# Attention of a three-stage kernel: the turned sums and rows of a pair behind the next pair's first scores, VectorE's work in another order, the scores' scale in the tanh, other first loads

## The chip, the cores and the metric

The kernel runs on one core of one Trainium2 chip. The metric is the time of one execution on the device in microseconds (us), lower is better; for each kernel the median of several runs is given. A profiled execution gives the trace, whose span is a little shorter than the run's time.

## The reference

Three stages follow each other: attention with a cap on the scores, a mixture of experts in which each token goes to one expert, and a soft mixture of experts.

```python
def _attn_ref(q, k, v, cap):                 # 4 x 12 heads, 448 positions, 64 wide
    scores = 1.0 / np.sqrt(q.shape[-1]) * np.matmul(q, k.transpose(0, 1, 3, 2))
    scores = cap * np.tanh(scores / cap)
    scores = scores - np.max(scores, axis=-1, keepdims=True)
    attn = np.exp(scores)
    attn = attn / (np.sum(attn, axis=-1, keepdims=True) + 1e-09)
    return np.matmul(attn, v)

def reference(...):
    x = attn_out.transpose(0, 2, 1, 3).reshape(1792, 768)
    x = _moe_ref(x, ...)       # logits = x @ w_gate + bias; argmax; gate * relu(x @ w1[e]) @ w2[e]
    return _moe2_ref(x, ...)   # softmax over tokens, 8 x 4 slots, experts, softmax over slots
```

## The kernel before

The work around the change is the first stage. The 48 heads are taken as 24 pairs (two heads of one batch item on 128 partitions), six pairs to each of the four batch items. The order of the instructions is written by hand in `attention` (L567): each engine runs its own instructions in the order in which this loop issues them, and semaphores make it wait for the others. Only the order within an engine can therefore be chosen, and a waiting instruction holds everything behind it on its engine, the transfers on SP's queue among them.

For pair p the steps are these.

- `load_qkv` (L754) loads q, k and v of pair p + 2 by SP's queue; pair 0 and 1 are loaded before the loop, with q of pair 0 on ScalarE's queue, behind the load of the cap (L1135).
- `split_qk` (L764) makes of q and k a high and a low part for the fp32r matmuls on VectorE, and multiplies q by `qsc`, which is 1 / (8 cap). `split(p + 1)` runs in pair p.
- `scores` (L591): the scores are made transposed (keys on partitions) in blocks of 128 keys, three matmuls to each product (high by high, high by low, low by high). Block 0 has its two PSUM banks "s"; block 1 uses banks s1 and s2, the small block of the last keys (c == NKC, both heads on one set of 128 partitions) s2, and block 2 s1 and s0. ScalarE takes the tanh of each (one instruction for block 0, one for the small block, two each for blocks 1 and 2: six a pair), and `pexp` (L607) the exponential of cap times that, in two instructions a pair.
- `scores1` does blocks 0 and 1, `scores2` the small block, `scores3` block 2.
- `pv` (L641) and `pv2` (L652) multiply the probabilities of pair p - 1 by v in the single bank "o"; `post1` (L655) copies the result from there.
- `adds1`, `adds2` add the blocks for the row sums on VectorE; `fold_rest` adds the small block too for the pairs in the set `quiet` (L694), which saves eight matmuls in `post2`.
- `post2` (L499) makes row sums and gate logits of pair p - 2 by narrow matmuls (r_ps, in the bank of `ps_m`), adds a guard on VectorE, and transposes the pair's result into the bank of `ps_x` (x_ps, L514). `post3` (L517) turns the sums (rt_ps, L520), takes reciprocals, scales the logits into `tmpg` and the rows into `xr`, which frees the bank of `ps_x`, and stores the rows to `x_dram`.
- `plan` (L678) puts the routing of a batch item (`route_batch`, L262: parts s0 to s3, of many short VectorE instructions and two matmuls for the ranks) at places (pair, 0 to 2) of the pairs behind its last rows; `route(p, place)` issues what is due. For the third batch item `route_first` and the gather for the first expert follow.
- `extra` (L660) places constants; in pairs 5 to 8 it sets the tile `xg` to zero on VectorE, which `zero_c` (L482) then stores.

The banks `s0` and "o" are also lent to routing (`Lent`, L663).

## Time and profile before

| | us |
|---|---|
| median of 3 runs | 496.83 (494.43 to 497.43) |
| the profiled execution | 496.84 |
| its span in the trace | 495.1 |
| TensorE (PE) busy | 458.5, 93% |
| VectorE (DVE) busy | 290.7, 59% |
| ScalarE (ACT) busy | 248.7, 50% |

Busy times are sums over instructions whose pipelines overlap, and an average over stages: the attention, up to about 200 us, is another mixture than what follows. A row of a timeline has the start, the duration, the engine, the source line, the operation, what it writes and reads with the shape, and how many instructions of a kind are drawn together; in brackets stands how long the engine had been idle before, and who ended that. PEld is TensorE's loading of weights, which runs beside its matmuls. "issue" means that no wait is seen.

### The profile page before, as it was taken

The page shows a single profiled execution, that of the slowest core. Times are in us where ns is not written, and L with a number is a line of the kernel's source. Part 1 is how long each engine was busy: PE and PEld are TensorE (multiplying, and loading weights), DVE is VectorE, ACT ScalarE, POOL GpSimd, SP SyncE. Part 2 cuts the span into 40 slices and gives each one's busy share as a digit, 9 for nine tenths or more (in the row PEclk, how much of TensorE's full clock was granted, in tenths as well). Part 3 has the DMA queues.
Part 4 walks back from the last instruction along what each step waited for, and adds up shares of the span by engine and source line. Part 5 has one row for each costly group of instructions (what it writes and reads, how often), then busy time and mean ns, then how long its engine had stood idle before and what let it go on. Part 6 is the DMA issues. An engine that isn't in the chain of part 4 may idle for free. (4 is left out here: it accounts for less than half of the span.)

```text
span 495.1 us, 10690 instructions
## 1 busy us (share of the span) xinstructions
PE 458.5 (93%) x4081; PEld 296.9 (60%) x4081; DVE 290.7 (59%) x738; ACT 248.7 (50%) x400; POOL 66.3 (13%) x140
## 2 busy tenths in 40 slices
PE   7999999999999989799998999999998979996773
PEld 5455555555555555588775888778876845542321
DVE  3899999999999995566652545245523323001323
ACT  4988968788798876333442335334432321100312
POOL 2100000000000004024331213121012103211000
PEclk9999999999999999899999999999999978999988
DMA  6356644665453405789949997988689899999997
GB/s 186 122 109 205 217 151 128 220 219 176 127 153 102 147 21 162 261 298 353 278 143 291 303 306 231 325 285 301 203 293 332 295 374 392 417 414 412 415 414 315
DMA packets 56214, 124.96 MB, mean 252 GB/s; under 512 B 9385, under 2 KB 25456, under 8 KB 56160
## 3 DMA queue, kind: packets, MB, share of 16 engines
q1 hardware_dynamic: 53696, 117.57, 68.9%
q0 software_dynamic: 2176, 6.44, 4.8%
q8 instruction: 33, 0.54, 0.4%
q10 hardware_dynamic: 288, 0.23, 0.2%
q14 instruction: 21, 0.17, 0.1%
HBM read 112.52 MB, written 11.71 MB: 251 GB/s over the span
## 5 line engine op out<-in xcount | busy, mean ns | idle before, releaser
L861 PE MATMUL acc_ps<-xh,wh 128*128 128x468 f32 x192 | 76.5, 399 | 1.7 <-DVEq L1260 0.9
L608 ACT ACTIVATE arena<-arena,capb 128x1792 f32<-128x1792 f32 (+1 forms) x48 | 77.0, 1604 | 1.6
L107 DVE TENSOR_TENSOR arena<-arena 128x896 f32<-128x896 f32 (+1 forms) x74 | 68.0, 919 | 9.8 <-ACT arena L608 8.0
L862 PE MATMUL acc_ps<-xl,wh 128*128 128x468 f32 x192 | 72.5, 378 | 0.0
L863 PE MATMUL acc_ps<-xh,wl 128*128 128x468 f32 x192 | 72.3, 377 | 0.0
L107 DVE TENSOR_TENSOR wl<-rw,wh 128x384 fp32r<-128x384 f32 x49 | 27.3, 559 | 74.4 <-ACT wh L814 61.7
L814 ACT CAST wh<-rw 128x384 fp32r<-128x384 f32 x64 | 32.3, 508 | 58.1 <-PE acc_ps L862 31.3
L649 PE MATMUL o_ps<-arena 128*64 128x448 f32 x288 | 59.6, 548 | 0.7 <-DVE arena L657 0.6
L605 ACT ACTIVATE arena<-s_ps 128x448 f32<-128x448 f32 x96 | 46.7, 541 | 10.3 <-PE s_ps L577 10.3
L470 POOL DMA_INDIRECT xg<-x_dram,idx x16 | 17.4, 1089 | 199.0 <-PE s_ps L577 171.0
L861 PEld LDWEIGHTS acc_ps<-xh,wh 128*128 128x128 f32 x192 | 36.5, 190 | 8.0 <-ACT wh L814 1.6
L863 PEld LDWEIGHTS acc_ps<-xh,wl 128*128 128x128 f32 x192 | 36.4, 190 | 5.3 <-DVE wl L107 0.6
L982 ACT ACTIVATE h<-acc_ps 128x468 f32<-128x468 f32 x32 | 18.0, 562 | 42.6 <-PE acc_ps L863 39.1
L862 PEld LDWEIGHTS acc_ps<-xl,wh 128*128 128x128 f32 x192 | 36.7, 191 | 3.6
L649 PEld LDWEIGHTS o_ps<-arena 128*64 128x64 f32 x288 | 18.4, 136 | 30.1 <-issue 18.9
L577 PE MATMUL s_ps<-qh,kh 64*128 64x448 f32 x144 | 32.1, 433 | 1.1 <-ACT arena L605 0.4
L577 PE MATMUL s_ps<-ql,kh 64*128 64x448 f32 x144 | 27.0, 364 | 0.2 <-DVE ql L113 0.2
L577 PE MATMUL s_ps<-qh,kl 64*128 64x448 f32 x144 | 26.9, 363 | 0.1
L107 POOL TENSOR_TENSOR wl<-rw,wh 128x384 fp32r<-128x384 f32 x15 | 15.6, 1043 | 72.5 <-ACT wh L814 49.0
L910 POOL DMA_INDIRECT c_dram<-cw,icur x16 | 16.1, 1004 | 56.7 <-DVE cw L107 42.8
L577 PEld LDWEIGHTS s_ps<-qh,kh 64*128 64x128 f32 x144 | 13.9, 183 | 16.1 <-ACT arena L605 8.9
L596 ACT ACTIVATE arena<-s_ps 128x896 f32<-128x896 f32 x24 | 21.6, 899 | 2.8 <-PE s_ps L577 2.8
(272 smaller groups left out, 743.3 us busy)
## 6 DMA issues: line engine op xcount, KB each, us to landing
ring<-in_moe_w_dram SPq DMA_DIRECT2D x30, 768.0 KB
w2r<-in_moe_w2t_dram SPq DMA_DIRECT2D x32, 384.0 KB
w2r<-in_moe_w_dram SPq DMA_DIRECT2D x28, 384.0 KB
arena<-in_moe_w_dram SPq DMA_DIRECT2D x13, 768.0 KB
rw<-in_moe_w_dram SPq DMA_DIRECT2D x24, 384.0 KB
arena<-in_moe_w_dram SPq DMA_DIRECT2D x22, 384.0 KB
kr<-in_k_dram SPq DMA_DIRECT2D x24, 256.0 KB
arena<-in_v_dram SPq DMA_DIRECT2D x24, 256.0 KB
```

Source lines behind the costliest of these rows:

```text
L107: (eng or nc.vector).tensor_tensor(out=out, in0=in0, in1=in1, op=op)
L470: nc.gpsimd.indirect_dma_start(out=xg[:, i, :], out_offset=None, in_=x_dram if rows is None else x_dram[:rows], in_offset=bass.IndirectOff ...
L577: nc.tensor.matmul(o, lhsT=kk[r, k], rhs=qq[r], start=(t == 0), stop=(t == 2))
L596: nc.scalar.activation(out=dst, in_=ps[:, :, :S], func=AF.Tanh)
L605: nc.scalar.activation(out=dst[:, h], in_=ps[h], func=AF.Tanh)
L608: nc.scalar.activation(out=t, in_=t, func=AF.Exp, scale=capb)
L649: nc.tensor.matmul(o[hd], lhsT=vt[:, c, hd], rhs=pt_t[p][:, c, h] if c < 2 else pt_m[p][:, 1 + h], start=(c == 0), stop=False)
L814: nc.scalar.copy(wh, rw)
L861: nc.tensor.matmul(ps, lhsT=wh, rhs=hi[k], start=(k == 0), stop=False)
L862: nc.tensor.matmul(ps, lhsT=wh, rhs=lo[k], start=False, stop=False)
L863: nc.tensor.matmul(ps, lhsT=wl, rhs=hi[k], start=False, stop=(k == total - 1))
L982: nc.scalar.activation(out=big["h"][n % NHB], in_=acc.pop(n), func=AF.Relu)
```

## The change

In the loop of a pair, the order becomes: scores1, fold_rest, the split of the next pair, the turn of the sums and rows of pair p - 3 (`finish`, pairs 3 to 18, its turned sums mostly in the lent bank s0), routing at place 0, pv, adds2, post2, pv2, the copy of the result (post1), routing at place 1, scores2, adds1, scores3, routing at place 2. From pair 18 on the turn of pair p - 2 also comes between scores2 and scores3, as before. The routing of the first two batch items moves one pair later, and `quiet` becomes 2, 3, 4, 6, 7, 8, 12, 13, 14, 18 (it was 2, 3, 4, 6, 7, 10, 11, 12, 13, 16, 17, 18, 19). The factor `qsc` leaves the split and becomes the scale operand of the six tanh. The zeros of `xg` come by four loads from the zero row of `x_dram`, on SP's queue. At the start q of pair 0 is issued ahead of the cap, v of pair 0 behind the loads of pair 1, the split of pair 0 ahead of the constants and with k in two halves; five matmuls warm TensorE up where seven did.

```diff
@@ -593,16 +593,16 @@
             if c == 0:
                 ps = ps_s.tile([128, 2, 512], F32, tag="s", name="s_ps")
                 product([ps[:, h, :S] for h in range(2)], k, p, by_heads)
-                nc.scalar.activation(out=dst, in_=ps[:, :, :S], func=AF.Tanh)
+                nc.scalar.activation(out=dst, in_=ps[:, :, :S], func=AF.Tanh, scale=qsc)
             elif c == NKC:
                 ps = bank(2, "sl_ps")
                 product([ps], k, p, together)
-                nc.scalar.activation(out=dst, in_=ps, func=AF.Tanh)
+                nc.scalar.activation(out=dst, in_=ps, func=AF.Tanh, scale=qsc)
             else:
                 ps = [bank(1, "s1_ps"), bank(2, "s1_ps")] if c == 1 else [bank(1, "s2_ps"), bank(0, "s2_ps")]
                 product(ps, k, p, by_heads)
                 for h in range(2):
-                    nc.scalar.activation(out=dst[:, h], in_=ps[h], func=AF.Tanh)
+                    nc.scalar.activation(out=dst[:, h], in_=ps[h], func=AF.Tanh, scale=qsc)
 
         def pexp(t):
             nc.scalar.activation(out=t, in_=t, func=AF.Exp, scale=capb)
@@ -658,7 +658,7 @@
             xun[p] = xt
 
         extra = {0: late_consts, 1: call(set_guard, 1e-9 * math.exp(-CAP_SMALL)), 2: later_consts, 4: last_consts}
-        extra.update({5 + i: call(nc.vector.memset, xg[:, i], 0.0) for i in range(NT)})
+        extra.update({5 + i: call(nc.sync.dma_start, xg_all[:, i], x_dram[NTOK].partition_broadcast(128)) for i in range(NT)})
         extra[9] = zero_c
         class Lent:
 
@@ -677,9 +677,10 @@
 
         def plan(b):
 
-            p, rb = (b + 1) * NP_ + 1, route_batch(b, a2p, lent_s)
-            at = [(p, 2), (p + 1, 1), (p + 1, 2), (p + 2, 1)]
-            if b == NB1 - 1:
+            early = b == NB1 - 1
+            p, rb = (b + 1) * NP_ + (1 if early else 2), route_batch(b, a2p, lent_s)
+            at = [(p, 2), (p + 1, 0), (p + 1, 2), (p + 2, 1 if early else 2)]
+            if early:
                 f0, f1, rest, sums_, turn = route_first(a2p, lent_s, lent_o)
                 rb += [f0, f1, sums_, rest, lambda: (turn(), gather(NA, NB1 * S))]
                 at += [(p + 1, 2), (p + 2, 2), (p + 3, 1), (p + 3, 1), (p + 3, 2)]
@@ -691,9 +692,16 @@
             for f in todo.pop((p, place), ()):
                 f()
 
-        quiet = set(range(2, LAST - 3)) - {5} - {(b + 1) * NP_ + 2 + i for b in range(NB1) for i in range(2)}
+        soon = NB1 * NP_
+        quiet = set(range(2, soon + 1)) - {NP_ - 1} - {(b + 1) * NP_ + 3 + i for b in range(NB1 - 1) for i in range(3)}
         n2 = 0
         spl[0] = first_split
+
+        def finish(q, pool=ps_m):
+            post3(q, a1, pool)
+            if q % NP_ == NP_ - 1 and q < soon:
+                plan(q // NP_)
+
         for p in range(NPAIR):
             if p + 2 < NPAIR:
                 raw[p + 2] = load_qkv(a1, a1q, p + 2)
@@ -701,9 +709,13 @@
                 m2_load(n2)
                 n2 += 1
             scores1(p)
-            route(p, 0)
             if p in quiet:
                 fold_rest(p - 2)
+            if p < LAST:
+                split(p + 1)
+            if 3 <= p <= soon:
+                finish(p - 3, ps_m if (p, 0) in todo else lent_s)
+            route(p, 0)
             if p >= 1:
                 pv(p - 1)
                 adds2(p - 1)
@@ -715,23 +727,19 @@
                 post1(p - 1)
                 post2(p - 2, a1, ps_x, ps_m)
                 break
-            split(p + 1)
             if p >= 2:
                 post2(p - 2, a1, ps_x, ps_m)
-            route(p, 1)
             if p >= 1:
                 pv2(p - 1)
+                post1(p - 1)
+            route(p, 1)
             scores2(p)
             adds1(p)
-            if p >= 1:
-                post1(p - 1)
-            if p >= 2:
-                post3(p - 2, a1, ps_m)
+            if p >= soon:
+                finish(p - 2)
             scores3(p)
             if p in extra:
                 extra[p]()
-            if p >= 2 and (p - 2) % NP_ == NP_ - 1:
-                plan((p - 2) // NP_)
             route(p, 2)
         assert not todo and n2 == NRING + 1 and a1.end <= UNIT * (NRINGA - 1)
         wsplits, xpreps, more_weights = item_start()
@@ -758,20 +766,22 @@
         vt = a1.tile([128, NKC + 1, 2 * HD], F32, tag="vt", name="vt", bufs=4)
         nc.sync.dma_start(kr, kT[b, hp])
         (eng or nc.sync).dma_start(qr, qT[b, hp].rearrange("h d s -> (h d) s"))
-        nc.sync.dma_start(vt, vP[b, hp])
-        return qr, kr, vt
-
-    def split_qk(a1q, qr, kr, act=False):
+        values = call(nc.sync.dma_start, vt, vP[b, hp])
+        if eng is None:
+            values()
+        return qr, kr, vt, values
+
+    def split_qk(a1q, qr, kr, first=False):
 
         qh, ql, kh, kl = (a1q.tile([128, w], F32R, tag=n, name=n, bufs=2)
                           for n, w in (("qh", S), ("ql", S), ("kh", S + KL), ("kl", S + KL)))
-        if act:
-            nc.scalar.copy(kh, kr)
-        else:
-            nc.vector.tensor_copy(kh, kr)
-        ts(qh, qr, qsc, ALU.mult)
-        stt(ql, qr, qsc, qh.bitcast(F32), ALU.mult, ALU.subtract)
-        tt(kl, kr, kh.bitcast(F32), ALU.subtract)
+        halves = [slice(0, 2 * KC), slice(2 * KC, S + KL)] if first else [slice(0, S + KL)]
+        for c in halves:
+            (nc.scalar.copy if first else nc.vector.tensor_copy)(kh[:, c], kr[:, c])
+        nc.vector.tensor_copy(qh, qr)
+        tt(ql, qr, qh.bitcast(F32), ALU.subtract)
+        for c in halves:
+            tt(kl[:, c], kr[:, c], kh[:, c].bitcast(F32), ALU.subtract)
         return qh, ql, kh, kl
 
 
@@ -1132,18 +1142,19 @@
             return ([call(wfirst, s) for s in range(AHEAD)], [call(xprep, k, "aat"[k % 3]) for k in range(KD)],
                     lambda: [w2load(j, e_first[-1]) for j in range(NR2)])
 
-        nc.scalar.dma_start(capt, cap.partition_broadcast(128))
         nc.vector.memset(bigf, 0.0)
         nc.vector.memset(xg_all[:, 0, :256], 0.0)
         first = {0: load_qkv(a1, a1q, 0, nc.scalar)}
+        nc.scalar.dma_start(capt, cap.partition_broadcast(128))
         nc.scalar.activation(out=bigf, in_=bigf, func=AF.Tanh)
 
         warm = ps_o.tile([128, S], F32, tag="o", name="warm")
         for _ in range(NWARM):
             nc.tensor.matmul(warm[:, :256], lhsT=xg_all[:, 0, :128], rhs=xg_all[:, 0, :256], start=True, stop=True)
+        first_split = split_qk(a1q, *first[0][:2], True)
         early_consts()
-        first_split = split_qk(a1q, *first[0][:2], act=True)
         first[1] = load_qkv(a1, a1q, 1)
+        first[0][3]()
         attention(a1, a1q, a2p, first, ps_s, ps_o, ps_x, ps_m, item_start)
 
     xh, xl, ps_a = big["xh"], big["xl"], big["ps", "a"]
@@ -1520,7 +1531,7 @@
         9], "pool": [4, 5]},
 }
 NRING = 5
-NWARM = 7
+NWARM = 5
 NRINGA = 12
 NRINGB = 5
 NRING2 = 9
```

## Rows read from the trace of the kernel before

**Rows 1.** Busy time by stretch: length, PE, PEld, DVE, ACT, POOL, PEclk, DMA share, GB/s.

```profile
43.00:66.00 23.00, 22.85 (x202) 12.88 (x200) 22.20 (x49) 19.30 (x25) 0.00 (x0) 1.00 0.54 169
434.00:480.00 46.00, 36.81 (x358) 14.09 (x350) 9.94 (x22) 7.39 (x16) 5.01 (x30) 0.93 1.02 414
```

**Rows 2.** Timeline of ScalarE, first tanh of pairs 0, 2, 5, 6, 7, 14, 15, 23.

```profile
8.68 0.92 ACT L596 ACTIVATE arena<-s_ps 128x896 f32<-128x896 f32 x1 [2.82 <-PE s_ps L577]
21.22 0.90 ACT L596 ACTIVATE arena<-s_ps 128x896 f32<-128x896 f32 x1
43.67 0.90 ACT L596 ACTIVATE arena<-s_ps 128x896 f32<-128x896 f32 x1
51.35 0.90 ACT L596 ACTIVATE arena<-s_ps 128x896 f32<-128x896 f32 x1
58.82 0.90 ACT L596 ACTIVATE arena<-s_ps 128x896 f32<-128x896 f32 x1
114.08 0.90 ACT L596 ACTIVATE arena<-s_ps 128x896 f32<-128x896 f32 x1
122.15 0.90 ACT L596 ACTIVATE arena<-s_ps 128x896 f32<-128x896 f32 x1
185.28 0.89 ACT L596 ACTIVATE arena<-s_ps 128x896 f32<-128x896 f32 x1
```

**Rows 3.** Timeline of PE and PEld in pair 6 and the start of pair 7.

```profile
55.17 0.36 PE L577 MATMUL sl_ps<-qh,kl 128*128 128x448 f32 x1
55.37 0.27 PE L520 MATMUL rt_ps<-ident,arena 128*112 128x128 f32 x1
55.88 0.37 PE L577 MATMUL s_ps<-ql,kh 64*128 64x448 f32 x2
57.08 0.18 PEld L577 LDWEIGHTS s_ps<-qh,kh 64*128 64x128 f32 x2 [0.40 <-ACT arena L605]
57.59 0.36 PE L577 MATMUL s_ps<-qh,kl 64*128 64x448 f32 x2
57.88 2.48 PE L649 MATMUL o_ps<-arena 128*64 128x448 f32 x12
```

**Rows 4.** Timeline of PE in the last pair, small and third block.

```profile
188.57 0.37 PE L577 MATMUL sl_ps<-qh,kl 128*128 128x448 f32 x1
189.18 0.36 PE L577 MATMUL s_ps<-ql,kh 64*128 64x448 f32 x2
```

**Rows 5.** Groups of ScalarE instructions, shapes apart: xcount | busy, mean ns | idle.

```profile
L877 ACT COPY htok<-h_ps 117x512 f32<-117x512 f32 x20 | 11.8, 591 | 15.1 <-PE h_ps L874 14.2
L1437 ACT ACTIVATE cT<-cT_ps,rs 96x512 fp32r<-96x512 f32 x3 | 2.0, 683 | 11.3 <-PE cT_ps L1435 11.3
L608 ACT ACTIVATE arena<-arena,capb 128x1792 f32<-128x1792 f32 x24 | 43.0, 1791 | 0.8
L608 ACT ACTIVATE arena<-arena,capb 128x1344 f32<-128x1344 f32 x24 | 34.0, 1417 | 0.8
```

**Rows 6.** Timeline of VectorE in pair 6, and of PE in pair 10.

```profile
50.62 2.33 DVE L107 TENSOR_TENSOR arena<-arena 64x448 f32<-64x448 f32 x3
57.83 0.70 DVE L236 MEMSET xg<- 117x768 f32 x1
88.14 0.32 PE L520 MATMUL rt_ps<-ident,arena 128*112 128x128 f32 x1 [0.41 <-DVE arena L110]
```

**Rows 7.** Timeline of PE, pairs 6 and 7.

```profile
54.02 0.92 PE L653 MATMUL o_ps<-arena 128*128 128x448 f32 x2
61.00 0.65 PE L514 MATMUL x_ps<-ident,arena 128*112 128x128 f32 x4
```

**Rows 8.** Groups of VectorE instructions, shapes apart, 10 to 165 us.

```profile
L107 DVE TENSOR_TENSOR arena<-arena 64x448 f32<-64x448 f32 x26 | 15.9, 611 | 0.4
```

**Rows 9.** Timeline of VectorE at the first split, of PE in pair 22.

```profile
6.33 0.45 DVE L110 TENSOR_SCALAR qh<-qr,qsc 128x448 fp32r<-128x448 f32 x1 [1.06 <-DMA qr<-in_q_dram]
179.63 0.81 PE L329 MATMUL tab_ps<-bsel,a 112*32 112x117 f32 x24
```

## What the change is predicted to do

> **What bounds the kernel now.** I read the busy table by stretches first, then the starts of the pairs on ScalarE, then TensorE and VectorE inside one pair.
>
> In the attention TensorE is without a gap: 22.85 of 23 us, with VectorE at 22.20 just behind it and ScalarE at 19.30 [rows 1]. The last weights come at the rate of the transfers: in 434 to 480 us the DMA engines are full while TensorE has 36.81 of 46 us [rows 1]. That stretch starts when earlier items free their buffers, so I let a microsecond of the attention count as one of the whole, and look for the change in the attention only.
>
> The first tanh of a pair is a good clock of the pairs. The 21 pairs from number 2 to number 22 last from 21.22 to 185.28, or 164.06 us [rows 2]. A quiet pair takes 7.47 (51.35 to 58.82), one whose sums are not folded 7.68 (43.67 to 51.35), one with the ranks of a batch 8.07 (114.08 to 122.15) [rows 2]. Pairs 0 and 1 take 12.54 together, 6.27 each: nothing old is turned in them yet, and ScalarE works through [rows 2].
>
> Inside a quiet pair TensorE has one real wait. The second block of the next pair's scores needs the bank that the tanh of this pair's third block empties: the weight load at 57.08 has been idle for 0.40, released by L605 [rows 3]. The chain is scores, tanh of head 0, scores; whatever lengthens one tanh lengthens the pair.
>
> Above 21 times 7.47 = 156.87 there are 7.2 us in these pairs. TensorE's own extra work explains: eight pairs not folded (5, 8, 9, 14, 15, 20, 21, 22) at 0.21, 1.7; the ranks of three batches at 8.07 - 7.47 - 0.21 = 0.39, 1.2; the table matmuls in pair 22, 0.8 [rows 2, 9]. About 3.5 us are left, and they are waits for VectorE's queue: so in a pair after routing, the turn of the sums starts at 88.14 after TensorE's load waited 0.41 on VectorE [rows 6].
>
> **The change part by part.** Times are against this execution, 496.84 us with a span of 495.1; the median shown, 496.83, is the same.
>
> *First loads.* VectorE begins the first split at 6.33, after 1.06 us of waiting for q alone [rows 9]. q was issued on ScalarE's queue behind the cap's load (128 tiny pieces) and beside v of pair 0; now q goes first, and v after pair 1. At best the whole 1.06 goes, at worst nothing (then k's arrival binds). From q to the first tanh was 8.68 - 6.33 = 2.35 [rows 2, 9]; the new order (split with k in halves, then three small constants, which the tanh now needs) is about as long, as an estimate. I take -0.9. Two warm-up matmuls fewer cost nothing: they end before q is there. Late next is the scale, made last on VectorE.
>
> *Scale in the tanh.* Six tanh of a pair now read a [128,1] scale. The nearest rows: a copy from PSUM of 512 columns without one takes 591 ns, one with a scale operand 683, so 92 more [rows 5]. Below, zero (hidden between back-to-back instructions); above, the exp, which has such a scale: 1791 for 1792 and 1417 for 1344 columns is 0.835 a column and 295 fixed, against 591 - 427 = 164 for the plain copy, 131 more, its source being SBUF too [rows 5]. I take 0.09, the like operation from the like memory. Where it counts:
> - pairs 0 and 1, bound by ScalarE: 2 x 6 x 0.09 = +1.1 (0 to 1.6);
> - the chain scores, tanh, scores in 21 pairs: 21 x 0.09 = +1.9 (0 to 2.7). There the next scores wait for the whole instruction, so nothing hides it.
>
> Elsewhere ScalarE has room: 19.30 of 23 us [rows 1].
>
> The Trainium skill, ScalarE: Activation LUTs, section What ACT_TABLE_LOAD costs, has 93 ns for each such operand and lets back-to-back activations overlap by as much. This trace agrees on the first (92); with the second rule carried to the chain the sum would lose the +1.9, which is the first rival below.
>
> In return qh and ql lose the scalar operand: still four instructions a pair, ql now of the kind that takes 0.61 for 448 columns [rows 8]. I count nothing; VectorE isn't the bound in a quiet pair.
>
> *The turn of the sums* (rt) leaves the place between the small block's scores and the third block's, and comes after the next pair's second block. Before: last small product 55.17, second product of the third block 55.88, 0.71. Without a turn between, in the last pair: 188.57 to 189.18, 0.61, so leaving saves 0.10 only [rows 3, 4]. At the new place scores to probabilities x V took 57.59 to 57.88, 0.29; with a turn, 0.20 (55.17 to 55.37) and then 0.20 to 0.29 more, 0.11 to 0.20 longer [rows 3]. Net 0.01 to 0.10; at 0.05 in the 15 pairs 3 to 17, +0.75. Pair 2 loses one turn and pair 18 gains it.
>
> *Fewer folds.* The set `quiet` loses 10, 11, 16, 17, 19 and gains 8, 14: three folds fewer, 3 x 0.21 = +0.6 on TensorE, and 3 x 2 x 0.61 = 3.7 us less on VectorE [rows 2, 8].
>
> *VectorE's order and load.* Four memsets of 0.7 each leave it (57.83 is one [rows 6]); SP issues four loads of a zero row in their place, each behind a store and ahead of the next pair's loads. These have most of two pairs until they are split, so I take nothing; if that cover were gone, a late k would hold the split, and then the next pair's scores. The folds, split and turned rows now run while VectorE would wait, and the copy of P x V comes ahead of the first add, which frees its bank early. Routing moves a pair later, into pairs without a fold. From all this I expect most of the 3.5 to go: -2.7, with 0.8 left where routing's chain is longest (bounds 0 and -3.5).
>
> *The new close place.* TensorE's x transposes of a pair (they follow the sums) need the PSUM bank that the rows' multiply frees; that multiply stood a whole pair ahead, and now stands in the same pair. From the end of pv2, 54.02 + 0.92 = 54.94, to the next x transposes, 61.00, are 6.06, and by the terms above 6.2 after [rows 7]. In it VectorE must do a whole pair's work but for adds2 and one short operation: 57.83 - 50.62 = 7.21, less 2.33 - 2 x 0.61 = 1.11, is at most 6.1 [rows 6, 8]. It fits, barely; I take 0.
>
> **The sum:** -0.9 + 1.1 + 1.9 + 0.75 + 0.6 - 2.7 = +0.75, or 496.84 + 0.75 = 497.6 us.
>
> **The rivals.**
> 1. The scale is hidden. For it: ScalarE often has its next instruction ready. Against: the 0.40 stands in every pair on a finished tanh [rows 3]. 497.6 - 1.1 - 1.9 = 494.6.
> 2. VectorE's waits don't go (the order only moves them): 497.6 + 2.7 = 500.3. For it: the work stays near the pair's length. Against: some 2.8 + 3.7 us leave VectorE altogether.
> 3. Slower: the rows' multiply comes after TensorE wants its bank. If VectorE's chain of 6.1 is in fact 6.8 beside the room of 6.2, each of the nine folded pairs from 3 on (18 among them) loses 0.6, 5.4 in all: 503.0. It decides from a chain of about 6.7 on. Against: 6.1 counts one operation too many.
> 4. All goes well: scale hidden (-3.0), all waits gone (-0.8), a free turn (-0.75), q the full 1.06 early (-0.16): 492.9. Only with a gain that I don't see would it pass 1%.
>
> **How the numbers follow.** About 1% (5 us) is what a measurement of this kernel can tell from no change. My forecast, near 497.6, gets 0.60; rival 1 0.13, rival 2 0.11, rival 3 0.08, rival 4 0.08, of which I put 0.07 below 491.9, since unseen gains lie there. So faster 0.07, same 0.85, slower 0.08. The range 493.3 to 501.0 holds the forecast with the bounds of its costs, rivals 1 and 2, and leaves out rival 3 and most of rival 4.
>
> **What would show it.** In the profile after: a tanh of 448 columns near 0.63, of 896 near 0.99; the first tanh near 7.8 us; pairs 0 and 1 near 6.8 each; a quiet pair near 7.6; pairs after routing without the extra 0.8 to 1.0; the load of the second block's scores still released by a tanh. I am wrong if a quiet pair stays at 7.47 or below (rival 1), if x transposes wait for VectorE (rival 3), if TensorE's granted clock falls in the attention, or if the stages behind it move by another amount than the attention does.

## The result and the profile after

The changed kernel takes 500.49 us in the median of 22 runs (497.25 to 505.44), the kernel before in the same rounds 497.02 (494.43 to 501.15): a ratio of 1.0067, 95% interval 1.0046 to 1.0087. One of the 22 executions, 505.44, lies more than 1.5% above the fastest, in a slower state, and the ratio leaves it out. The kernel is slower by 3.5 us, inside the 1% that the prediction took as no change, and inside its range (493.3 to 501.0); but the forecast, 497.6, was 2.9 us too low.

The profiled execution of the changed kernel took 504.16 us with a span of 502.4. That is 3.7 us above its own median, so its trace shows more than the change. A second trace of the same kernel, from the run e12_after_again below (500.46 us, span 498.7), is put beside it wherever the two differ.

The busy line of the page, first trace (busy us, share of the span, instructions of each engine):

```profile
PE 463.4 (92%) x4101; PEld 299.9 (60%) x4101; DVE 283.6 (56%) x729; ACT 262.1 (52%) x401; POOL 67.4 (13%) x140
```

VectorE lost 7.1 us of work and ScalarE gained 13.4, nearly all of it the tanh's; neither says by itself what became of the time.

ScalarE's first tanh of a pair is the clock of the pairs again (start, duration, engine, line, operation, shapes; in brackets the idle time before and who ended it). The first fence is the first trace of the kernel after: pairs 0, 2, 7, 8, 9, 10, 20, 21, 23. The second is its second trace: pairs 0, 1, 2, 23.

```profile
7.24 1.01 ACT L596 ACTIVATE arena<-s_ps,qsc 128x896 f32<-128x896 f32 x1 [1.83 <-DVE qsc L110]
21.60 0.99 ACT L596 ACTIVATE arena<-s_ps,qsc 128x896 f32<-128x896 f32 x1
...
60.11 0.99 ACT L596 ACTIVATE arena<-s_ps,qsc 128x896 f32<-128x896 f32 x1
67.82 0.99 ACT L596 ACTIVATE arena<-s_ps,qsc 128x896 f32<-128x896 f32 x1
75.53 0.99 ACT L596 ACTIVATE arena<-s_ps,qsc 128x896 f32<-128x896 f32 x1
84.41 0.99 ACT L596 ACTIVATE arena<-s_ps,qsc 128x896 f32<-128x896 f32 x1
...
163.58 0.99 ACT L596 ACTIVATE arena<-s_ps,qsc 128x896 f32<-128x896 f32 x1
173.37 0.99 ACT L596 ACTIVATE arena<-s_ps,qsc 128x896 f32<-128x896 f32 x1
...
190.08 0.99 ACT L596 ACTIVATE arena<-s_ps,qsc 128x896 f32<-128x896 f32 x1
```

```profile
7.08 1.01 ACT L596 ACTIVATE arena<-s_ps,qsc 128x896 f32<-128x896 f32 x1 [1.78 <-DVE qsc L110]
13.89 0.99 ACT L596 ACTIVATE arena<-s_ps,qsc 128x896 f32<-128x896 f32 x1
20.68 0.99 ACT L596 ACTIVATE arena<-s_ps,qsc 128x896 f32<-128x896 f32 x1
...
189.14 0.99 ACT L596 ACTIVATE arena<-s_ps,qsc 128x896 f32<-128x896 f32 x1
```

Against [rows 2]: the first tanh comes 1.44 to 1.60 us earlier; pairs 0 and 1 take 14.36 in the first trace and 13.60 in the second, where 12.54 stood; pairs 2 to 22 take 168.48 and 168.46, where 164.06 stood. A quiet pair takes 7.71 instead of 7.47 (60.11 to 67.82). Pair 9 with the first ranks takes 8.88 (75.53 to 84.41), pair 20 with the third 9.79 (163.58 to 173.37).

The tanh themselves, grouped by form (xcount | busy, mean ns of one | idle before): first the line of the kernel before for the 448 columns, then the kernel after.

```profile
L605 ACT ACTIVATE arena<-s_ps 128x448 f32<-128x448 f32 x96 | 46.7, 541 | 10.3 <-PE s_ps L577 10.3
```

```profile
L605 ACT ACTIVATE arena<-s_ps,qsc 128x448 f32<-128x448 f32 x96 | 55.4, 629 | 4.9 <-PE s_ps L577 4.9
L596 ACT ACTIVATE arena<-s_ps,qsc 128x896 f32<-128x896 f32 x24 | 23.7, 989 | 1.8 <-DVE qsc L110 1.8
L600 ACT ACTIVATE arena<-sl_ps,qsc 128x448 f32<-128x448 f32 x24 | 15.2, 635 | 16.4 <-PE sl_ps L577 16.4
```

A tanh of 448 columns went from 541 to 629 ns, one of 896 from 0.90 us [rows 2] to 0.989: the 0.09 of the sum.

TensorE in pair 6 and at the start of pair 7, kernel after, as [rows 3] before:

```profile
56.39 0.36 PE L577 MATMUL sl_ps<-qh,kl 128*128 128x448 f32 x1
...
56.99 0.36 PE L577 MATMUL s_ps<-ql,kh 64*128 64x448 f32 x2
...
58.28 0.18 PEld L577 LDWEIGHTS s_ps<-qh,kh 64*128 64x128 f32 x2 [0.49 <-ACT arena L605]
58.79 0.37 PE L577 MATMUL s_ps<-qh,kl 64*128 64x448 f32 x2
59.09 0.32 PE L520 MATMUL rt_ps<-ident,arena 128*112 128x128 f32 x1
59.34 2.48 PE L649 MATMUL o_ps<-arena 128*64 128x448 f32 x12
```

Two things are to be seen. The wait of the weight load on the tanh of the third block is 0.49 instead of 0.40. And from the last product to the probabilities x V are 0.55 us, where 0.29 stood [rows 3]: 0.30 to the turn, 0.25 after it.

The ranks of a batch now stand ahead of the probabilities x V on TensorE. The kernel after at pair 9 and at pair 20:

```profile
75.25 0.35 PE L285 MATMUL rank_ps<-oh,tri 112*112 112x32 f32 x2 [0.42 <-DVE ex L107]
...
164.09 0.35 PE L285 MATMUL rank_ps<-oh,tri 112*112 112x32 f32 x2 [1.47 <-DVE ex L107]
164.57 2.48 PE L649 MATMUL o_ps<-arena 128*64 128x448 f32 x12
```

At both TensorE waits for the routing on VectorE (L107), 0.42 and 1.47 us by its own record, and everything behind it waits as well.

Last, pair 0. TensorE's granted clock in 9 to 11 and 11 to 14 us (busy time of PE, PEld, DVE, ACT, POOL with instructions, then clock, DMA share, GB/s), first trace and then second trace of the kernel after:

```profile
9.00:11.00 2.00, 1.65 (x5) 1.06 (x7) 0.04 (x1) 1.97 (x2) 0.00 (x0) 0.53 0.87 235
11.00:14.00 3.00, 3.00 (x20) 2.18 (x22) 2.75 (x9) 2.32 (x5) 1.07 (x2) 0.74 0.68 220
```

```profile
9.00:11.00 2.00, 1.80 (x13) 1.45 (x15) 0.08 (x1) 1.97 (x3) 0.00 (x0) 1.00 0.93 253
11.00:14.00 3.00, 2.44 (x18) 1.10 (x16) 2.90 (x9) 2.97 (x5) 1.22 (x2) 1.00 0.73 250
```

In the first trace the clock was near its lower level (1.2 of 2.4 GHz) and pair 0 took 7.57; in the second it stayed full and pair 0 took 6.81 (7.08 to 13.89). So 0.76 of the first trace belong to the clock of one execution, and not to the instructions.

### The profile page after: what moved, and what is told of

The parts are those of the page before. It is cut to its first block, busy times and chain, and to the rows that moved or that the text cites. A ratio compares the mean times of both kernels' runs of the same rounds, so it can differ in the third digit from the quotient of the medians.

```text
span 502.4 us, 10749 instructions
## 1 busy us (share of the span) xinstructions
PE 463.4 (92%) x4101; PEld 299.9 (60%) x4101; DVE 283.6 (56%) x729; ACT 262.1 (52%) x401; POOL 67.4 (13%) x140
## 5 line engine op out<-in xcount | busy, mean ns | idle before, releaser
L107 DVE TENSOR_TENSOR wl<-rw,wh 128x384 fp32r<-128x384 f32 x49 | 27.3, 559 | 73.4 <-ACT wh L824 60.1
L107 DVE TENSOR_TENSOR arena<-arena 128x896 f32<-128x896 f32 (+1 forms) x68 | 63.5, 945 | 6.3 <-ACT arena L608 5.9
L605 ACT ACTIVATE arena<-s_ps,qsc 128x448 f32<-128x448 f32 x96 | 55.4, 629 | 4.9 <-PE s_ps L577 4.9
L107 POOL TENSOR_TENSOR wl<-rw,wh 128x384 fp32r<-128x384 f32 x15 | 15.6, 1043 | 72.5 <-ACT wh L824 72.5
L596 ACT ACTIVATE arena<-s_ps,qsc 128x896 f32<-128x896 f32 x24 | 23.7, 989 | 1.8 <-DVE qsc L110 1.8
L600 ACT ACTIVATE arena<-sl_ps,qsc 128x448 f32<-128x448 f32 x24 | 15.2, 635 | 16.4 <-PE sl_ps L577 16.4
```

Source lines behind the costliest of these rows:

```text
L107: (eng or nc.vector).tensor_tensor(out=out, in0=in0, in1=in1, op=op)
L596: nc.scalar.activation(out=dst, in_=ps[:, :, :S], func=AF.Tanh, scale=qsc)
L605: nc.scalar.activation(out=dst[:, h], in_=ps[h], func=AF.Tanh, scale=qsc)
```

## The experiments

One table first, worked out from the traces of all runs (times in us; the ratio against the kernel before in the same rounds with its 95% interval; "quiet" is the median of pairs 3, 4, 6, 12, 13; "end" is the start of the first expert's products, when the attention and its tail are over). Each line is one trace, and the runs were made on several chips: e1 to e4 on one in the same rounds, so too e5 to e7, e8 and e9, e10 and e11; the ratio compares with before in those rounds, the traces all with the one trace of before.

| | ratio | first tanh | pairs 0, 1 | quiet | pair 9 | pair 20 | pairs 2 to 22 | end | span |
|---|---|---|---|---|---|---|---|---|---|
| before | 1 | 8.68 | 12.54 | 7.48 | 7.67 | 8.07 | 164.06 | 203.64 | 495.1 |
| after, first trace | 1.0067 (1.0046 to 1.0087) | 7.24 | 14.36 | 7.70 | 8.88 | 9.79 | 168.48 | 209.02 | 502.4 |
| e12_after_again | 1.0069 (1.0042 to 1.0097) | 7.08 | 13.60 | 7.71 | 8.87 | 9.78 | 168.46 | 207.38 | 498.7 |
| e1_scale_only | 1.0033 (0.9998 to 1.0068) | 8.50 | 13.59 | 7.57 | 7.75 | 8.18 | 164.94 | 206.49 | 496.0 |
| e2_ranks_late | 1.0022 (0.9991 to 1.0054) | 7.27 | 14.37 | 7.72 | 8.88 | 8.50 | 167.37 | 207.90 | 499.3 |
| e3_turn_back | 1.0097 (1.0061 to 1.0133) | 7.29 | 13.62 | 7.58 | 11.50 | 9.79 | 170.17 | 210.16 | 501.3 |
| e4_filled_start | 1.0070 (1.0034 to 1.0106) | 7.03 | 13.67 | 7.71 | 8.87 | 11.41 | 170.07 | 209.96 | 499.6 |
| e5_order_only | 0.9889 (0.9840 to 0.9937) | 8.93 | 12.55 | 7.48 | 8.47 | 8.41 | 162.79 | 203.28 | 493.2 |
| e6_ranks_pair_later | 1.0018 (0.9972 to 1.0065) | 6.96 | 13.61 | 7.71 | 8.04 | 8.51 | 169.13 | 208.44 | 498.1 |
| e7_combined | 0.9861 (0.9816 to 0.9906) | 7.35 | 13.11 | 7.49 | 8.48 | 8.40 | 162.95 | 202.17 | 492.2 |
| e8_scale_back | 1.0083 (1.0047 to 1.0119) | 9.19 | 13.41 | 7.60 | 8.88 | 11.48 | 168.99 | 210.27 | 501.3 |
| e9_zeros_only | 0.9993 (0.9953 to 1.0034) | 8.43 | 12.54 | 7.48 | 7.67 | 8.08 | 162.76 | 202.40 | 495.7 |
| e10_zeros_start | 0.9944 (0.9912 to 0.9975) | 6.96 | 13.04 | 7.49 | 7.66 | 8.07 | 162.81 | 202.05 | 490.3 |
| e11_combined_again | 0.9898 (0.9848 to 0.9947) | 7.02 | 13.13 | 7.48 | 8.50 | 8.42 | 162.88 | 201.90 | 489.2 |

**e1, the scale alone.** The kernel before with the scale in the tanh and without it in the split, in all three tanh lines.

```diff
-nc.scalar.activation(out=dst, in_=ps[:, :, :S], func=AF.Tanh)
+nc.scalar.activation(out=dst, in_=ps[:, :, :S], func=AF.Tanh, scale=qsc)
...
-ts(qh, qr, qsc, ALU.mult)
-stt(ql, qr, qsc, qh.bitcast(F32), ALU.mult, ALU.subtract)
+nc.vector.tensor_copy(qh, qr)
+tt(ql, qr, qh.bitcast(F32), ALU.subtract)
```

> The kernel before with one part of the change alone: qsc leaves the split and becomes the scale operand of the six tanh of a pair. Theory (a scale operand lengthens each tanh by 0.09 us, and the second block's scores wait for a whole tanh): a tanh of 448 columns 0.63 us, a quiet pair 7.56 instead of 7.47, the 21 pairs 2 to 22 take 164.06 + 1.9 = 166.0 us, pairs 0 and 1 together 12.54 + 1.1 = 13.6 us, the whole +3 us. Rival (the operand's cost is hidden by ScalarE's overlap, and the longer pair of the changed kernel comes from the turn's new place alone): 164.1 and 12.5 us, the whole unchanged.

Measured: pairs 0 and 1 are 1.05 us longer, a quiet pair 0.09 longer; pairs 2 to 22 only 0.88, since a part of the longer pair is taken from waits for VectorE (pair 10 fell from 8.46 to 8.15). So the scale shows in full in pairs 0 and 1 and in the quiet pairs, and only in part where VectorE is waited for: the first rival, a hidden scale, falls, and so does a cost of 0.09 in each of the 21 pairs. The whole is 1.0033 (medians 498.18 against 497.83), not clear of no change and less than the 3 us expected.

**e2, the ranks later in the pair.** The kernel after with the ranks at place 1, behind pv2, instead of place 0, ahead of pv.

```diff
-at = [(p, 2), (p + 1, 0), (p + 1, 2), (p + 2, 1 if early else 2)]
+at = [(p, 2), (p + 1, 1), (p + 1, 2), (p + 2, 1 if early else 2)]
```

> The changed kernel with the ranks of a batch (part s1 of the routing) issued at place 1 of their pair, behind pv2, instead of place 0, ahead of pv. Theory (at place 0 TensorE's rank matmuls stand ahead of pv while VectorE is still making the one-hot matrix that they read, behind the adds of the pair before): pairs 9, 15 and 20 fall from 8.88, 8.81 and 9.79 us to about 8.3, the 21 pairs 2 to 22 from 168.5 to about 165.8 us, the whole -2.6 us. Rival (these pairs are long because of the routing work on VectorE itself, wherever the matmuls stand): no more than 0.5 us less in all.

Measured: pair 20 falls by 1.29 (9.79 to 8.50), but pairs 9 and 15 stay at 8.88 and 8.81. TensorE in pair 9 of this run:

```profile
79.55 0.29 PE L285 MATMUL rank_ps<-oh,tri 112*112 112x32 f32 x2
...
80.66 0.47 PE L577 MATMUL s_ps<-qh,kh 64*128 64x448 f32 x1
81.28 0.44 PE L577 MATMUL s_ps<-qh,kh 64*128 64x448 f32 x1 [0.15 <-DVE rk L107]
```

The ranks don't wait for VectorE any more; but they stand in the lent bank s0, and by this edit the turned sums of that pair do too (they keep the other bank only where ranks stand at place 0). The third block's scores of the second head, which need s0, start 0.62 behind those of the first (80.66 to 81.28), and the record names VectorE as what ended the last 0.15. So one wait took the place of another in part; these rows don't show where all of the unchanged 8.88 goes. In pair 20 the turn is at the old place again and not in s0; it shows the gain alone.

**e3, the turn at its old place.** The kernel after with post3 of pair p - 2 between the small block and the third block, in all pairs.

```diff
-            if 3 <= p <= soon:
-                finish(p - 3, ps_m if (p, 0) in todo else lent_s)
...
-            if p >= soon:
+            if p >= 2:
                 finish(p - 2)
```

> The changed kernel with the turn of the sums and the rows' multiply (finish) of pair p - 2 between the scores of the small and the third block in all pairs, as before the change, and nothing behind the next pair's first scores; the ranks stay at place 0. Theory (a turn costs TensorE about 0.16 us more at its new place than at its old one): a quiet pair falls from 7.71 to about 7.55 us, the 21 pairs 2 to 22 from 168.5 to about 166.1 us. Rival (the quiet pair is long because of the tanh alone, the place of a turn is worth 0.05 us or less): 7.66 us and about 167.7 us.

Measured: a quiet pair falls from 7.71 to 7.58, so the new place of the turn costs 0.13. But pair 15 rises to 9.77 and pair 9 to 11.50: with less work on TensorE ahead of the ranks it waits longer for VectorE there (1.53 us at pair 9), and behind that wait the granted clock fell to 0.50 in 76 to 78 us. The whole is slower than the change itself. The turn's price is shown; that it decides the whole is not.

**e4, TensorE's first wait filled.** The kernel after with five products of x in pair 0 while TensorE waits for the first tanh.

```diff
+            if p == 0:
+                w2 = ps_o.tile([128, S], F32, tag="o", name="warm2")
+                for _ in range(5):
+                    nc.tensor.matmul(w2[:, :256], lhsT=xg_all[:, 0, :128], rhs=xg_all[:, 0, :256], start=True, stop=True)
```

> The changed kernel with five more fp32 matmuls of 256 columns, whose results nobody reads, in pair 0 between its first scores and its small block's. Theory (with the earlier first tanh TensorE stands still for 2 us before the small block's scores, its granted clock falls to 0.53 in 9 to 11 us, and that lengthens pair 0): the granted clock stays at 1.00 there and pair 0 takes about 6.8 us instead of 7.57, the whole -0.7 us. Rival (pair 0 is long because ScalarE waits in its own order, not because of the clock): pair 0 stays at 7.5 us.

Measured: pair 0 takes 6.89 at full clock, where the first trace of the change had 7.57; but the second trace of the change has 6.81 with nothing filled in. The whole is unchanged, 1.0070. So the 0.7 is the clock's, and it doesn't come in each execution: of the five traces of kernels with the early first tanh and no filling (after, e12, e2, e3, e6) two show the fall (after, e2), of the four with it (e4, e7, e10, e11) none. Whether the filling prevents it can't be told from nine traces. Pair 20 of this run shows the other place where the clock falls:

```profile
163.16 0.38 PE L285 MATMUL rank_ps<-oh,tri 112*112 112x32 f32 x2 [1.47 <-DVE ex L107]
...
163.85 3.90 PE L649 MATMUL o_ps<-arena 128*64 128x448 f32 x12
```

```profile
164.00:166.00 2.00, 2.00 (x6) 0.62 (x8) 1.90 (x8) 1.97 (x3) 0.00 (x0) 0.50 0.73 265
```

The wait is the 1.47 of the kernel after, but then the clock is 0.50, the probabilities x V take 3.90 instead of 2.48, and pair 20 takes 11.41 instead of 9.79.

**e5, the order without turn, early ranks, scale and first loads.** The kernel after with e2's and e3's edits, without the scale in the tanh, and with load_qkv, split_qk and the first loads of before. What stays of the change is VectorE's order, the later routing, the new set `quiet`, and the zeros by transfer.

Beside the edits shown at e2 and e3, and in all three tanh lines:

```diff
-nc.scalar.activation(out=dst, in_=ps, func=AF.Tanh, scale=qsc)
+nc.scalar.activation(out=dst, in_=ps, func=AF.Tanh)
...
-NWARM = 5
+NWARM = 7
```

> Of the change only the order of VectorE's work, the fewer folds, the later routing and the zeros by transfer; the scale is back in the split, the first loads are those of before, the turn stands between the small and the third block, the ranks at place 1. Theory (what the change lost are the scale in the tanh, the turn's new place and the ranks' place, and the order itself takes VectorE's waits away): a quiet pair 7.48 us, the first pair with ranks about 8.2, the 21 pairs 2 to 22 about 162.4 us where before has 164.06, pairs 0 and 1 12.5 us; the whole -1.5 us against before. Rival (the waits of before are not to be had by this order, it only moves them): 164 us or more, the whole unchanged against before.

Measured: faster than before, 0.9889; pairs 2 to 22 in 162.79, pair 9 at 8.47, pair 15 at 8.40, pair 20 at 8.41. Against e8 below, which differs from this kernel in the places of the turn and the ranks alone, pairs 9 and 15 are 0.41 and 0.42 shorter, 0.13 of it the price of the turn that other pairs show too; e2 alone left them where they were, and e3 alone made them longer. That is the interplay that e2 and e3 could not show, some 0.3 us in each of these two pairs. A pair with ranks at 8.40 to 8.47 is still 0.3 to 0.4 longer than with the routing of before (8.07 in e9).

**e6, the ranks a whole pair behind the one-hot.** The kernel after with the first two batches' ranks at place 0 of pair p + 2 and the parts behind them a pair later too; the third batch's ranks are at place 1, as in e2.

```diff
-at = [(p, 2), (p + 1, 0), (p + 1, 2), (p + 2, 1 if early else 2)]
+at = [(p, 2), (p + 1, 1), (p + 1, 2), (p + 2, 1)] if early else [(p, 2), (p + 2, 0), (p + 2, 2), (p + 3, 2)]
```

> The changed kernel, but for the first two batch items the ranks (s1) come a whole pair behind the one-hot matrix, at place 0 of pairs 10 and 16, with s2 and s3 one pair later too; for the third at place 1 of pair 20. Theory (the matmuls of the ranks waited for a one-hot matrix made too late; a pair later it is ready): pairs 9 and 15 take 7.9 us instead of 8.88 and 8.81, pairs 10 and 16 8.3 instead of 7.9, pair 20 8.5 instead of 9.79; the 21 pairs 2 to 22 166.2 us instead of 168.5. Rival (the place of the ranks is no cause; they cost the same 0.6 us over TensorE's work wherever they stand, by holding the bank s0 or VectorE): pairs 10 and 16 take 8.8 and 167.3 us in all.

Measured: pairs 9 and 10 together take 16.28 instead of 16.78, pairs 15 and 16 16.19 instead of 16.72. But pairs 12 and 18 rise to 9.22 and 9.33, and there TensorE waits at a place where of the other runs only e8 shows a wait, of 0.2 in pairs 11 and 17; this is pair 12, VectorE's multiply of the rows and TensorE's transposes:

```profile
101.72 0.68 DVE L107 TENSOR_TENSOR arena<-x_ps,arena 112x512 f32<-112x512 f32 x1
...
102.55 0.62 PE L514 MATMUL x_ps<-ident,arena 128*112 128x128 f32 x4 [1.47 <-DVE arena L107]
```

This is the third rival's mechanism: the last part of the routing came ahead of a folded pair, VectorE's rows' multiply became late, and the x transposes wait for their bank, 1.47 us. The ratio, 1.0018, tells it neither from before nor clearly from the change.

**e7 and e11, a combination.** e5 with the new first loads, the scale as the tanh's operand in pair 0 alone, and the filling of e4; e11 is the same kernel again.

Beside the edits shown at e2, e3 and e4, with split_qk multiplying by qsc from pair 1 on:

```diff
-func=AF.Tanh, scale=qsc)
+func=AF.Tanh, **({"scale": qsc} if p == 0 else {}))
```

> The order of e5 with the changed kernel's first loads; the scale operand only in the six tanh of pair 0, in the split for all other pairs; five filler matmuls in pair 0, whose results nobody reads. Theory: first tanh at 7.2 us instead of 8.68, pair 0 6.9 us, pair 1 6.3, a quiet pair 7.48 us, the 21 pairs 2 to 22 about 162.4 us; against before -1.5 for the order and -0.8 for the start, the whole about -2.3 us. Rival (what the start gains is given back in the first pairs, which ScalarE bounds): the 23 pairs end no earlier than in e5.

> The earlier combination once more, unchanged, on the chip and in the rounds of the run beside it. Its trace showed an attention only 1.5 us shorter than before's, while its times were 6 us lower. Theory: the rest behind the attention, whose instructions are the same, differs from execution to execution by up to 4 us, and the true gain is nearer to what the pairs show: ratio 0.993 to 0.997. Rival: the gain is real and repeats (0.984 to 0.990); then something outside the pairs' times that the profiled execution did not show carries it.

Measured: 0.9861 and 0.9898, with e5's 0.9889 the fastest here, in the median 492.87 and 493.05 where before stood at 498.85 and 497.20 in the same rounds. The first tanh comes at 7.35 and 7.02, pairs 0 and 1 take 13.1, pairs 2 to 22 162.9. That is an attention that ends 1.5 to 1.7 us earlier, while the whole is 4 to 6 us faster, and e11 repeats this gain, as its rival theory had it. Against e10 of the same rounds (0.9944, an attention 0.15 longer) the intervals overlap, so what the order adds to zeros and start is not told apart from nothing.

**e8, the scale back in the split.** The kernel after without the scale in the tanh, with load_qkv, split_qk and the first loads of before, since the early first split needs the scale in the tanh.

```diff
-nc.scalar.activation(out=dst, in_=ps, func=AF.Tanh, scale=qsc)
+nc.scalar.activation(out=dst, in_=ps, func=AF.Tanh)
```

> The changed kernel with the scale back in the split (so no scale operand in the tanh) and, since the split then needs the scale, the first loads of before; order, turn and ranks as changed. Theory (in this order VectorE no longer hides part of the scale's cost, so it counts in full in each pair): a quiet pair 7.62 instead of 7.71 us, the 21 pairs 2 to 22 about 168.5 - 1.9 = 166.6 us, pairs 0 and 1 12.5 instead of 14.4 us; the whole -2 us against the changed kernel. Rival (in the changed order something else than the tanh releases the second block's scores): a quiet pair stays at 7.7 us.

Measured: a quiet pair falls to 7.60, by 0.11. But the whole is 1.0083, no better than the change: the first tanh is back at 9.19, pairs 0 and 1 took 13.41 where 12.5 was expected, with a granted clock of 0.59 in 11 to 14 us, and pair 20 took 11.48 as in e4. The early ranks and the early turn remain, and they carry the loss. Against e5, which differs in those two alone, pairs 2 to 22 are 6.2 us longer, some 1.7 of it the clock in pair 20.

**e9, the zeros alone.** The kernel before with the four memsets replaced by four transfers.

```diff
-extra.update({5 + i: call(nc.vector.memset, xg[:, i], 0.0) for i in range(NT)})
+extra.update({5 + i: call(nc.sync.dma_start, xg_all[:, i], x_dram[NTOK].partition_broadcast(128)) for i in range(NT)})
```

> The kernel before with the four memsets replaced by the four loads of the zero row, nothing else. Theory (the gain of the order in e5, 1.3 us in the 21 pairs, comes only in part from these): pair 7 falls from 7.77 to 7.48 us, pair 8 from 8.92 to about 8.5, the rest stays, the 21 pairs 2 to 22 163.3 us instead of 164.06. Rival (the loads, each behind a store on SP's queue, hold up the loads of q and k): a pair between 5 and 9 gets longer; or (the memsets were all of the gain) 162.8 us.

Measured: pairs 2 to 22 take 162.76, as in e5. ScalarE's starts of pairs 8 and 9, before, and then here:

```profile
66.59 0.90 ACT L596 ACTIVATE arena<-s_ps 128x896 f32<-128x896 f32 x1
75.51 0.90 ACT L596 ACTIVATE arena<-s_ps 128x896 f32<-128x896 f32 x1
```

```profile
66.03 0.90 ACT L596 ACTIVATE arena<-s_ps 128x896 f32<-128x896 f32 x1
74.10 0.90 ACT L596 ACTIVATE arena<-s_ps 128x896 f32<-128x896 f32 x1
```

Pair 8 falls from 8.92 to 8.07, pair 7 from 7.77 to 7.49; 1.3 us in all 21 pairs, so the rival that the memsets were all of the gain came true. By the pairs' times the other order of VectorE, the later routing and the new set of folds in e5 bring nothing on balance beyond the memsets. By the whole time e5 seems to have more: 0.9889 against 0.9993 here, two intervals that don't meet; but the two were measured in different rounds, and what that is worth stands under what stays open.

**e10, zeros and start.** e9 with load_qkv, split_qk and the first loads of e7, the scale in pair 0's tanh, and the filling shown at e4.

```diff
-func=AF.Tanh)
+func=AF.Tanh, **({"scale": qsc} if p == 0 else {}))
...
-NWARM = 7
+NWARM = 5
```

> The kernel before with three edits: the gates' memsets of pairs 2 to 21 replaced by the four transfers of zero rows at the start, the first loads of the changed kernel (with the scale as the tanh's operand in pair 0 alone), and five products of x in pair 0 that fill TensorE's first wait. VectorE's order and the turn stay as before. Theory: what the earlier combination gained in the attention came from these edits: first tanh at about 7.3, pairs 0 and 1 together 13.1, pairs 2 to 22 together 162.8, so the attention ends about 2.5 us earlier than before and the whole is 1.5 to 3 us faster (ratio 0.994 to 0.997). Rival: VectorE's order brings something that the pairs' times do not show; then this kernel stays near 0.999 and the combination near 0.986.

Measured: 0.9944. The first tanh comes at 6.96, pairs 0 and 1 take 13.04, pairs 2 to 22 162.81, so the last pair starts 2.5 us earlier (182.81 against 185.28), and the end comes 1.6 earlier, since what follows the last pair took 0.9 longer in this trace. So the attention explains 1.6 to 2.5 of the gain of 2.6 us in the median (494.56 against 497.20).

**e12, the change again.** No edit.

> The changed kernel itself once more, for a second trace of it. Its profiled execution took 504.16 us, 3.7 above its median. Theory: what was read in the pairs is fixed by the order of the instructions and comes back within 0.1 us: first tanh at 7.2, pair 0 at 7.6 with the granted clock fallen, quiet pairs 7.71, pairs 9 and 15 at 8.8 to 8.9; only pair 20 (7.9 to 11.4 in its variants) and the time behind the attention (287 to 294 in the traces so far) differ, so the whole is 500 to 501 in the median, ratio 1.005 to 1.009. Rival: the long pair 0 or the 7.71 belonged to that one execution; then pair 0 takes 6.9 or quiet pairs 7.6.

Measured: pairs 2 to 22 come back within 0.02 us, pair 20 too: what was read in the pairs is in the order of the instructions. Pair 0 is the exception, 6.81 at full clock, so its length in the first trace belonged to that execution. The median is 501.00 against 497.68, +3.3.

## Why the forecast was near and where it failed

The right "no change" stood on a sum of which several terms were wrong, the waits for VectorE most of all. The second trace, whose clock stayed full, is set against [rows 2] here, with the experiments for the terms that one trace can't separate:

| term | forecast | measured | from |
|---|---|---|---|
| first loads | -0.9 | -1.6 | 7.08 against 8.68 |
| scale, pairs 0 and 1 | +1.1 | +1.06 | 13.60 against 12.54 |
| scale in the chain, 21 pairs | +1.9 | +0.9 to +2.1 | 0.88 in all (e1); 0.09 (e1) to 0.11 (e8) in a quiet pair, times 21 |
| turn's new place, 15 pairs | +0.75 | +2.0 | 0.13 each (e3; its pairs 9 and 15 have other waits) |
| three folds fewer | +0.6 | +0.6 | 7.90 against 7.71 in pair 5 |
| waits for VectorE | -2.7 | -0.3 to +0.9 | the rest of 168.46 - 164.06 = 4.40, with 2.1 or 0.9 for the scale |
| last pair's start | +0.75 | +3.86 | 189.14 against 185.28 |

The end of the attention moved by +3.7 (207.38 against 203.64), the span by +3.6, the medians by +3.3 to +3.5: for the change itself a microsecond of the attention counted as one of the whole, as assumed. For other runs it did not; that stands under what stays open.

**First loads: right way, too small.** Kernel after, VectorE's first split, as [rows 9] before:

```profile
4.53 0.40 DVE L781 CAST qh<-qr 128x448 fp32r<-128x448 f32 x1 [3.20 <-DMA qr<-in_q_dram]
...
6.60 0.15 DVE L110 TENSOR_SCALAR capb<-capt 128x1 f32<-128x1 f32 x1 [0.34 <-DMA capt<-in_cap_dram]
...
6.99 0.15 DVE L110 TENSOR_SCALAR qsc<-qsc 128x1 f32<-128x1 f32 x1
```

"At best the whole 1.06 goes" was no bound: a wait behind one queue bounds what that wait can give, not how much earlier q can land when it is issued first. Before, VectorE was making the scale until 5.27 and only the rest of q's way showed as a wait. The split starts 1.80 earlier (4.53 against 6.33), and 0.36 of that goes into the way from the split to the first tanh, 2.71 (4.53 to 7.24) where "about as long" as 2.35 was put in. "Late next is the scale" was right: the cap's load, now behind q, sets the time of the scale and so ends the wait of the first tanh. One small reading was off: the warm-up matmuls of before end at 6.70 by the trace, after q's arrival, and not before it.

**The scale: right in place and for one tanh, too large in the sum.** The chain scores, tanh, scores of the prediction's first section carries it: the weight load behind the tanh waits 0.49 instead of 0.40, and a quiet pair of e1 is 0.09 longer, one operand of its six. But "nothing hides it" holds for the quiet pairs only. In pairs that wait for VectorE the longer tanh takes the place of waiting: e1's 21 pairs are 0.88 longer together, and between e8 and e12, which differ by the scale and the first loads, 20 of them (without pair 20, whose clock differs) by 1.17 (157.51 to 158.68). The figure of the Trainium skill, ScalarE: Activation LUTs, section What ACT_TABLE_LOAD costs (93 ns for each pointer operand) agrees with 541 to 629 ns; its overlap of back-to-back activations hides none of it in the chain of a quiet pair, where TensorE needs the finished tanh.

**The turn: the mis-sized term.** The saving at the old place came as predicted: 56.39 to 56.99 is 0.60, against 0.71 [rows 3]. At the new place 0.11 to 0.20 was put in, taken from the turn behind the small block's product; there it costs 0.26 (0.55 - 0.29). The small block's products use all 128 rows of the array, and the turn behind them started 0.20 later; the second block's use 64 rows for each head, and the turn behind them starts 0.30 later. The row for that was there: what followed the same product before came 0.29 later (57.59 to 57.88 [rows 3]). That the rows of the array are the reason is not shown. The net of 0.13 to 0.15 lay outside the bounds of 0.01 to 0.10 that were meant to hold it.

**VectorE's waits: the failed step.** "From all this I expect most of the 3.5 to go" is not what happened: in the sum of the pairs between 0.3 of them are gone and 0.9 have come. The memsets gave 1.3 (e9 alone shows it). The later routing and the order give an estimated 0.6, since e5 takes as long as e9 with three folds fewer. Of these 1.9 most, or more than all, was taken back, most visibly at one place that the prediction passed over: place 0 in the changed plan holds not only VectorE's routing but TensorE's two rank matmuls, ahead of pv in TensorE's order, and they need the routing that VectorE has only just begun. Pairs 9, 15 and 20 take 8.87, 8.80 and 9.78 where 7.71 + 0.2 + 0.39 = 8.3 would be the pair by the prediction's own terms: 2.55 us together. The runs show some 1.8 of it to be the place of ranks and turn: 1.28 in pair 20 (e2), and 0.28 each in pairs 9 and 15, beyond the turn's 0.13 (e5 against e8). The cause of the rest is open. Where the change could add a wait was asked of VectorE's rows' multiply, and not of the first TensorE instruction that a moved part of the routing issues.

**The rivals.** The hidden scale (494.6) is refuted by e1 and e8. "VectorE's waits don't go" came nearest, 500.3 against 500.5, and its core is true: the order moved the waits. The agreement of the number is partly luck, since the turn cost 1.25 more than it assumed, while the first loads gave 0.7 more and the scale cost up to 1.0 less. The same holds for the forecast: had the first loads given only the 0.9, the time would have been some 501.2, above the range. Late rows (503.0) are not in the change, whose x transposes follow the logits without a wait; e6 shows the mechanism, from a small shift of the routing. That the granted clock could fall in the attention was written down as a sign of being wrong, but given no price: it fell in pair 0 of one of two traces (0.76), in pair 20 of e4 and e8 (1.6 to 1.7), in pair 0 of e2 and e8, and in pair 9 of e3.

**What stays open.** Behind the attention the instructions are the same, but in these fourteen traces that part takes 287.3 (e11) to 293.4 (after, first trace). Some of it is the granted clock of the execution: in e9 it was 0.83 in 240 to 260 us, where before had 1.00. And most runs are faster in the median, against before in their rounds, than their attention in the trace explains: e5, e7 and e11 by 2.4 to 4.5 us (e5 -4.1 us, with an attention that ends 0.4 earlier), but so are e1 to e4 and e6 by 2.4 to 3.7, some of it the clock in their traces. The rounds of e5 can be looked at from within: there e6 is 5.5 us slower than e5 and e7 1.8 faster, and their attentions end 5.2 later and 1.1 earlier. So inside these rounds the attention explains the times within some 0.7 us, and what is left over lies in the comparison with before, whose median was 498.85 there and 497.02 to 498.54 elsewhere, and of which there is one trace only. That e5's order has a gain which the pairs don't show is therefore not shown; a trace of before from the same rounds, which no run gives, would decide it.

## What to carry to other kernels

Moving a step in a hand-written order moves all that it issues on every engine: look first for the one instruction on the bounding engine, here two small rank matmuls, and ask whether its input is ready at the new place. Two moves that share a bank can each look of little use alone (e2, e3) and be worth several microseconds together (e5 against e8: 6.2 in the pairs, 1.7 of it the clock). A [128,1] operand on an activation costs its full time where a chain runs through it, and nothing where the engine has room: of the six of a quiet pair one counted, in pairs 0 and 1, where ScalarE sets the pace, nearly all. So it belongs into the one pair where it lets the start come earlier (e7), not into all.

## What was not expected of the hardware

The same wait of TensorE does not have the same price in each execution. At pair 20, second trace of the change, then e8:

```profile
163.15 0.27 PEld L285 LDWEIGHTS rank_ps<-oh,tri 112*112 112x112 f32 x2 [1.81 <-ACT arena L608]
163.18 0.35 PE L285 MATMUL rank_ps<-oh,tri 112*112 112x32 f32 x2 [1.46 <-DVE ex L107]
...
163.66 2.48 PE L649 MATMUL o_ps<-arena 128*64 128x448 f32 x12
```

```profile
164.08 0.35 PE L285 MATMUL rank_ps<-oh,tri 112*112 112x32 f32 x2 [1.56 <-DVE ex L107]
...
164.56 4.17 PE L649 MATMUL o_ps<-arena 128*64 128x448 f32 x12
```

The rank matmuls wait 1.46 or 1.47 us in both traces of the change and in e4, behind a weight load that has been idle for 1.8, and 1.56 in e8. In both traces of the change the clock stays at 1.00 and the probabilities x V take 2.48; in e4, with the same instructions at this place, it falls to 0.50 and they take 3.90, in e8 4.17. In pair 0 a wait of 2.0 us cost 0.76 in one trace of the change and nothing in the other. So a wait of this size is to be priced with two numbers, and a single trace can show either.
